# Four layers of linear attention and gated MLP, forward and backward: other orders at the seams of the forward pass, and the last output stored in quarters

## The chip, the core and the metric

The kernel runs on one core of a Trainium2 chip. That core has a matrix engine (TensorE, "PE" in the profile, with its weight loads as "PEld"), a vector engine (VectorE, "DVE"), a scalar engine (ScalarE, "ACT"), GpSimd ("POOL"), and SyncE ("SP"), which issues the DMA transfers. The engines run side by side, each through its own list of instructions in order, and wait for one another on semaphores. Results of matrix products land in PSUM, a small memory that other engines must read before a tile of it can be written again.

The metric is the time of one execution on the device in microseconds (us); what is compared is the median over executions.

## The reference

A sequence of 2048 rows of width 512 in bf16 goes through four blocks, attention, MLP, attention, MLP, with the same weights in both pairs. The output is the forward result and the gradients of the input and of five weights.

```python
def attn(x, wqkv, wo):                 # 32 heads of 16
    q, k, v = split(x @ wqkv)
    phi = lambda t: where(t > 0, t + 1, exp(t)) + 1e-6
    pq, pk = phi(q), phi(k)
    kv  = einsum("bhsd,bhse->bhde", pk, v)     # one 16x16 matrix for each head
    z   = einsum("bhsd->bhd", pk)
    num = einsum("bhqd,bhde->bhqe", pq, kv)
    den = einsum("bhqd,bhd->bhq", pq, z) + 1e-6
    return (num / den) @ wo
def mlp(x, wg, wu, wd):                # inner width 1376
    return (sigmoid(x @ wg) * (x @ wu)) @ wd

x = A_x
x = x + attn(layernorm(x)); x = x + mlp(layernorm(x))
x = x + attn(layernorm(x)); x = x + mlp(layernorm(x))
# outputs: x, and vjp(grad_out) for A_x, wqkv, wo, w_gate, w_up, w_down
```

No row can begin its attention output before the sums over all 2048 rows, kv and z, are known. So each attention has a stage that makes keys and queries of all rows, and then a stage that applies them.

## The kernel before

**Tiles.** The rows are cut into 16 tiles (`st`, 0 to 15) of 128; two neighbours form a pair (`i`, 0 to 7), four a block. The residual of every tile stays in SBUF (`k.xs`, f32). A matrix product needs its left operand with the contracted dimension on partitions, so normed rows (`h`) and normed queries (`pqn`) must be turned, in one of two ways: TensorE multiplies the 128x128 blocks by an identity into PSUM and VectorE or ScalarE copies the result to SBUF, or SyncE issues a transposing DMA from SBUF to SBUF (L1020) or from DRAM.

**Who sets the order.** The forward pass is inside a `tc.manual_schedule` for TensorE, ScalarE, VectorE and GpSimd: each of these runs its instructions in the order in which the program calls them. The order of SyncE's queue, with its loads and stores, is made by a planner. PSUM tiles come from five pools: `t`, `g` and `u` with two buffers each, `y` and `ln` with one. A matmul that takes a new tile from a pool waits until the older tile in that buffer has been read.

**Stages.** Two layer pairs follow one another, each made of `kq_fwd` (key stage and start of the attention) and `ab_fwd` (the rest of the attention, and the MLP). Then comes the backward pass, which is not touched but for its last products.

*`kq_fwd`.* For each tile: key projection (TensorE, `t_mm`), `exp_to` (ScalarE), `clamp` and `phi_out` (VectorE, the latter reads the PSUM tile and writes `pk_all`), the same for the query, then partial sums of kv. It needs the turned normed rows. In the first layer pair they are turned as it goes (`stage_hT`). In the second (l = 2) tiles 0 and 1 were turned at the end of the MLP before (`early_T`, L611), tiles 2 and 3 are turned by `stage_hT([2, 3], "vector")` in the middle of tile 0's keys, tiles 4 and 5 by `put_hT([4, 5], "vector")` in the middle of tile 2's (both with VectorE's copy from PSUM, L379), and the later ones by DMA from DRAM (`load_hT`). The turned rows are also stored for the backward pass (`store_hT`).

After the last tile the stage makes kv (`kvbdT`), folds it with wo to M (`M_sb`, four products, each copied from PSUM by ScalarE or VectorE in turn), and begins the attention of the first tiles.

*The fronts of the attention* (`attn_fronts`, L960 on). For a tile: `prod` (query times z), `front1` (VectorE's reduction to `den`), `front2` (reciprocal and `pqn`, in the buffer `pqnstage`), `front3` (four blocks turned by TensorE into the one `ln` PSUM buffer, copied by ScalarE to `pqnT`), then `attn_mm` (four products of `pqnT` with `M_sb` into `y_ps`) and `attn_add` (VectorE adds it to the residual and takes statistics for the next norm). Tiles 0 to 3 go one by one. From pair 2 on the fronts work on pairs: `pair_prod` (GpSimd), `pair_front1`, `pair_front2`. For pairs 3 to 7 `pair_front2` has `pqn` turned by two DMAs (L1020). For pair 2 (tiles 4 and 5) it is called with `turned=False`, and `pair_front3(2)` (L1033) has TensorE turn eight blocks, copied by ScalarE in one piece.

*`ab_fwd`.* The prologue takes the MLP of tiles 0 and 1 one tile at a time, with the attention of tiles 2 and 3 in between. `gu(st, nt, c0, nch)` is one unit: gate and up products (L1133, into `g_ps` and `u_ps`), two sigmoids by ScalarE, `hhT` by VectorE (which reads `u_ps`), one product by GpSimd (`ssd_t`, L1152) and its store (L1155). `stage_T` turns normed rows of coming tiles. `fill` and `fills` turn parts of the weights for the backward pass, as work for TensorE with a copy behind it. Then a loop over pairs 1 to 7 has six units per pair (`CUNITS`), with the attention of the next pair, `pair_front1` and `pair_front2` of pairs further on, and `down_mm` (the down product of a tile, L1168, followed by the residual's add and the statistics) between the units. So the turned queries of pair 2 are first used in the loop's first round (i = 1), by the attention of tiles 4 and 5 behind its first unit.

At the end, with a next layer pair to come (`nxt`): turned rows of tiles 0 and 1 (`early_T`), norm of tile 13, down product of tile 14, a block transpose by VectorE (`trans`, STREAM_TRANSPOSE in the trace), down product of tile 15, another block transpose.

*The end of the kernel.* `p2_gen` makes the weight gradients as jobs; each job is four units (`ic`, 0 to 3) of 16 matmuls into a `p_ps` tile (L1778); VectorE adds to it a part that was stored earlier, into `dw_stg`, and after the fourth unit the whole 128x4x256 result goes out in one DMA (L1732, in the helper `io`). Between the last units the main program takes steps of `a_small_grads`, which makes the small gradients of the attention weights (`sg_ps`, copied by ScalarE to `fin_o` at L2157 and stored at L2158). Its last step comes after the last unit.

## Time and profile before

| | |
|---|---|
| three executions | 1104.79, 1104.92, 1106.0 us |
| median | 1104.92 us |
| the profiled execution's own time | 1104.22 us |
| span of its profile | 1102.5 us |
| granted TensorE clock in it | 1.00 |
| busy: TensorE / VectorE / ScalarE / GpSimd | 1076.6 / 719.1 / 484.9 / 463.1 us |
| second key stage begins | 202.0 us |
| last unit of the weight gradients released to VectorE | 1097.84 us |

The span runs from the first to the last instruction of the profile; the execution's time also has what lies around it, here 1.7 us. Positions below are microseconds from the span's start. A line of a timeline gives the start, the duration, the engine, the program's line, the operation, output and inputs by their names, the shapes, a count where several equal instructions follow one another, and in square brackets the time for which the engine stood idle just before, with the instruction that released it. "SPq" is an instruction in SyncE's queue, so a DMA's line there is its issue, not its landing.

### The profile page before, as it was taken

How to read it: one execution, taken by the hardware profiler on the slowest of the kernel's cores; microseconds unless marked ns; L12 is line 12 of the kernel's file. 1: busy time of each engine (PE TensorE's matmuls, PEld its weight loads, DVE VectorE, ACT ScalarE, POOL GpSimd, SP SyncE). 2: the span in 40 equal slices, each digit the busy share in tenths (PEclk: the TensorE clock that was granted, in tenths of full speed). 3: DMA queues.
4: the chain of work that ended last, by engine and by line, in shares of the span. 5: the costliest groups of instructions: out<-in, count | busy, mean ns of one | idle time of the engine just before them, and what ended most of it. 6: DMA issues, size and time to landing. Idle time of an engine off the chain costs nothing. (4 is left out here: it accounts for less than half of the span.)

```text
span 1102.5 us, 19826 instructions
## 1 busy us (share of the span) xinstructions
PE 1076.6 (98%) x7255; PEld 660.9 (60%) x7356; DVE 719.1 (65%) x1257; ACT 484.9 (44%) x907; POOL 463.1 (42%) x631
## 2 busy tenths in 40 slices
PE   8999999999999999999999999999999999999998
PEld 4477777447777744445756556544447755555587
DVE  7798997878888667777965620067778946632221
ACT  6676555547555524444633441234346513420001
POOL 5637776435765447773101420048881102420000
PEclk9999999999999999999999999999999999999999
DMA  8948997796797688976899968898869999958997
GB/s 260 318 150 216 249 251 231 208 251 155 219 290 230 188 273 287 300 237 209 244 269 258 273 212 283 253 334 250 233 189 247 272 256 264 263 184 285 266 253 168
DMA packets 365330, 269.55 MB, mean 244 GB/s; under 512 B 132464, under 2 KB 339760, under 8 KB 365232
## 3 DMA queue, kind: packets, MB, share of 16 engines
q1 hardware_dynamic: 365232, 268.28, 85.3%
q8 instruction: 57, 0.93, 0.3%
q14 instruction: 41, 0.34, 0.1%
HBM read 122.62 MB, written 119.47 MB: 220 GB/s over the span
## 5 line engine op out<-in xcount | busy, mean ns | idle before, releaser
L1778 PE MATMUL p_ps<-p_set,p_a 128*128 128x384 bf16 (+2 forms) x1792 | 264.4, 303 | 1.5 <-DMA p_set<-sv_hdd 0.8
L1778 PEld LDWEIGHTS <-p_a 128*128 128x128 bf16 x1792 | 168.8, 96 | 85.0 <-PE p_ps L1778 1.0
L1469 POOL TENSOR_TENSOR dd<-dhb,ssd 128x512 bf16<-128x512 bf16 x84 | 97.0, 1158 | 102.9 <-ACT dhb L1467 96.3
L1468 DVE TENSOR_TENSOR dd<-dhh_ps,ssd 128x512 bf16<-128x512 f32 x85 | 57.2, 679 | 119.9 <-ACT dhb L1467 117.1
L1493 PE MATMUL dh_ps<-wuT,dd 128*128 128x512 bf16 (+1 forms) x339 | 128.5, 379 | 0.5
L1493 PE MATMUL dh_ps<-wgT,dd 128*128 128x512 bf16 (+1 forms) x329 | 124.7, 379 | 0.1
L1493 PEld LDWEIGHTS <-dd 128*128 128x128 bf16 x680 | 66.4, 98 | 79.6
L1152 POOL TENSOR_TENSOR ssd_t<-hhT,oms 128x512 bf16<-128x512 bf16 (+2 forms) x76 | 82.8, 1098 | 49.1 <-DVE hhT L1151 22.4
L1793 DVE TENSOR_TENSOR dw_stg<-p_ps,dw_stg 128x384 bf16<-128x384 f32 (+2 forms) x76 | 32.2, 438 | 105.6 <-PE p_ps L1778 96.7
L1467 ACT CAST dhb<-dhh_ps 128x512 bf16<-128x512 f32 x84 | 48.7, 589 | 115.4 <-PE dhh_ps L1461 108.1
L1133 PE MATMUL u_ps<-hT,wu 128*128 128x256 bf16 (+1 forms) x792 | 92.7, 261 | 1.2 <-DVE hhT L1151 1.0
L1133 PE MATMUL g_ps<-hT,wg 128*128 128x256 bf16 (+1 forms) x792 | 92.8, 261 | 0.7 <-DVE den L972 0.4
L1090 DVE STREAM_TRANSPOSE tr_stg<-dd 128x768 f32<-128x768 f32 (+1 forms) x62 | 86.8, 1435 | 1.5 <-DMA sv_hdd<-tr_stg 0.4
L1133 PEld LDWEIGHTS <-wg 128*128 128x128 bf16 x792 | 70.1, 98 | 17.0 <-issue 0.5
L1461 PE MATMUL dhh_ps<-gT,wdT 128*128 128x512 bf16 x299 | 76.9, 379 | 2.2 <-DVE dd L1468 1.5
L1168 PE MATMUL y_ps<-wd,hhT 128*128 128x512 bf16 (+1 forms) x337 | 77.7, 379 | 0.8
L1133 PEld LDWEIGHTS <-wu 128*128 128x128 bf16 x792 | 70.6, 98 | 9.0 <-issue 2.1
L1149 ACT ACTIVATE ssd_t<-g_ps 128x512 bf16<-128x512 f32 (+2 forms) x76 | 42.5, 559 | 63.2 <-PE g_ps L1133 60.6
L1795 ACT CAST dw_stg<-p_ps 128x384 bf16<-128x384 f32 (+2 forms) x76 | 28.1, 386 | 84.1 <-PE p_ps L1778 80.9
L1461 PEld LDWEIGHTS <-wdT 128*128 128x128 bf16 x352 | 34.2, 98 | 43.3 <-issue 3.5
L1151 DVE TENSOR_TENSOR hhT<-u_ps,ssd_t 128x512 bf16<-128x512 f32 (+2 forms) x76 | 47.2, 629 | 17.8 <-PE u_ps L1133 11.0
L1150 ACT ACTIVATE oms<-g_ps 128x512 bf16<-128x512 f32 (+2 forms) x96 | 53.7, 559 | 10.0 <-POOL ssd_t L1152 9.3
(256 smaller groups left out, 1879.8 us busy)
## 6 DMA issues: line engine op xcount, KB each, us to landing
sv_hdd<-tr_stg SPq DMA_DIRECT2D x72, 384.0 KB, 4.8
p_set<-sv_hdd SPq DMA_DIRECT2D x18, 1536.0 KB, 7.3
ssd<-sv_ssd SPq DMA_DIRECT2D x23, 768.0 KB, 5.2
sv_ssd<-ssd_t SPq DMA_DIRECT2D x61, 256.0 KB, 3.4
h_ld<-sv_h SPq DMA_DIRECT2D x30, 256.0 KB, 4.0
sv_hdl<-tr_stg SPq DMA_DIRECT2D x24, 256.0 KB, 5.1
p_a<-sv_h SPq DMA_DIRECT2D x12, 512.0 KB, 6.7
p_set<-sv_hdl SPq DMA_DIRECT2D x24, 256.0 KB, 5.0
```

The lines of the kernel that those rows point to most:

```text
L1090: nc.vector.transpose(t[:, :, 0:n * P].bitcast(F32).rearrange("p q (a j) -> p q a j", a=2 * n), src.rearrange("p c x -> p (c x)").bitcast( ...
L1133: nc.tensor.matmul(ps[:, ci * n:(ci + 1) * n], lhsT=w_sb[:, kc, (c0 + ci) * P:(c0 + ci + 1) * P], rhs=hT[:, kc, (st % 2) * P:(st % 2) * P ...
L1150: nc.scalar.activation(oms, gv, ACT.Sigmoid, scale=-1.0)
L1151: nc.vector.tensor_tensor(hh, uv, ssd[:, :, 0, :], ALU.mult)
L1152: nc.gpsimd.tensor_tensor(ssd[:, :, 1, :], hh, oms, ALU.mult)
L1168: nc.tensor.matmul(y_ps[:], lhsT=h[0:r, fc, off:off + P], rhs=k.wd[0:r, fc, :], start=(fc == 0), stop=(fc == NFC - 1))
L1461: nc.tensor.matmul(ps[:], lhsT=k.wdT[:, jc, u * P:(u + 1) * P], rhs=self.gT[B][:, jc, :], start=(jc == 0), stop=(jc == NDC - 1))
L1467: nc.scalar.copy(dhb[:], ps[:])
L1468: nc.vector.tensor_tensor(self.dd[ng][:, 0, c, :], ps[:], self.ssd[ng][:, c, 0, :], ALU.mult)
L1469: nc.gpsimd.tensor_tensor(self.dd[ng][:, 1, c, :], dhb[:], self.ssd[ng][:, c, 1, :], ALU.mult)
L1493: nc.tensor.matmul(self.acc[j][:], lhsT=dd[0:r, a, c, j * P:(j + 1) * P], rhs=w[0:r, u, :], start=(u == 0 and a == 0), stop=(u == NFC - 1 ...
L1778: nc.tensor.matmul(ps[:, 0:w], lhsT=lhs[:, s, ic * P:(ic + 1) * P], rhs=rhs, start=(s == 0), stop=(s == NST - 1))
```

## The change

It is made of these parts.

1. **Tiles 2 and 3 of the second key stage** are turned at the end of the MLP before, between the down products of tiles 14 and 15 (`early_T(1, "scalar")`), with the copy on ScalarE; the turn in the key stage is gone. `down_mm` is split so that the residual's add can be called by itself, and the end of `ab_fwd` is reordered: block transpose, down product of tile 14, turn, add, block transpose, down product of tile 15.
2. **Tiles 4 and 5 of the second key stage** are turned where they were, but copied by ScalarE.
3. **Attention tile 1** is turned after the four products for M, not before them, and copied by VectorE.
4. **In the prologue of `ab_fwd`** one weight turn (`fills(1)`) goes ahead of `front3(3)`.
5. **The queries of tiles 4 and 5** are turned by two DMAs, like those of later pairs; `pair_front3` is removed. In the first round of the loop their attention stands behind the second unit, not the first. The add of tile 0's down product goes behind tile 1's last unit.
6. **The last output** of the weight gradients leaves in four stores of 64 KB, one behind each unit, and the last step of `a_small_grads` comes ahead of the last unit.

Parts 3, 4 and 5 occur twice, once in each layer pair.

```diff
@@ main, the end of the kernel
         for i in range(last):
+            if i == last - 1:
+                next(sg, None)
             next(w2)
-            if i % 2 == 1:
+            if i % 2 == 1 and i < last - 1:
                 next(sg, None)
...
-    def early_T(self):
+    def early_T(self, pair, evac):
         k = self.k
         hT = k.lnres["hT"].tile([P, NDC, 2, P], BF16, name="hT")
-        self.transposes(hT[:], (0, 1), "vector")
-        k.nc.sync.dma_start(out=k.sv[self.l]["hT"][0, :, :], in_=hT[:].rearrange("p c n t -> p (c n t)"))
-        for st in range(2):
-            self.early[st] = hT[:, :, st, :]
+        self.transposes(hT[:], (2 * pair, 2 * pair + 1), evac)
+        k.nc.sync.dma_start(out=k.sv[self.l]["hT"][pair, :, :], in_=hT[:].rearrange("p c n t -> p (c n t)"))
+        for j in range(2):
+            self.early[2 * pair + j] = hT[:, :, j, :]
...
@@ kq_fwd
             if l == 2 and st == 0:
                 load_hT(1, (1,))
-                stage_hT([2, 3], "vector")
             elif l == 2 and st == 2:
                 hTs["cur"] = hTq[1]
-                put_hT([4, 5], "vector")
+                put_hT([4, 5], "scalar")
...
         A.prod(2, nc.vector)
         A.front1(2)
-        A.front3(1)
         phis.append(late_q(NST - 1))
         for c in range(NDC):
             m_ps = ps_tile(k, "gu"[c % 2], [P, D], F32, "M_ps")
             nc.tensor.matmul(m_ps[:], lhsT=kvbdT[:, c, :], rhs=k.wo[:, c, :], start=True, stop=True)
             evac_copy(k, A.M_sb[:, c, :], m_ps[:], "vector" if c % 2 else "scalar")
         nc.scalar.activation(k.tab[:], k.neg[:], ACT.Sigmoid)
+        A.front3(1, "vector")
         A.attn_y(0)
...
@@ pair_front2 (pair_front3 is removed)
-        if turned:
-            pqnT = pool.tile([P, 2, NDC, P], BF16, name="pqnT2", bufs=2)
-            for j in range(2):
-                nc.sync.dma_start_transpose(out=pqnT[:, j, :, :], in_=pqn[:, j, :])
-                F_[2 * i + j] = dict(T=pqnT[:, j, :, :])
+        pqnT = pool.tile([P, 2, NDC, P], BF16, name="pqnT2", bufs=2)
+        for j in range(2):
+            nc.sync.dma_start_transpose(out=pqnT[:, j, :, :], in_=pqn[:, j, :])
+            F_[2 * i + j] = dict(T=pqnT[:, j, :, :])
         nc.sync.dma_start(out=dram_batch(sva["pqn"], i, 2), in_=pqn[:])
...
@@ ab_fwd, prologue
         gu(0, 1, *CQUADS[2])
+        fills(1)
         A.front3(3)
-        fills(1)
         gu(1, 1, *CQUADS[0], between=lambda: A.attn_y(3, "t"))
         ln.apply(2)
         A.pair_front1(2)
         gu(1, 1, *CQUADS[1])
         ln.apply(3)
-        A.pair_front2(2, False)
+        A.pair_front2(2)
         A.pair_prod(3)
-        down_mm(0)
+        add = down_mm(0)
         gu(1, 1, *CQUADS[2])
+        add()
         turn_weights()
         ln.stage_T([2, 3], bank="t")
         fill("gu", "scalar")
-        A.pair_front3(2)
...
@@ ab_fwd, loop
             gu(st, 2, *CUNITS[0])
             if l == 3 and i > 1:
                 turn_weights()
-            A.attn_y(st + 2, "t")
-            A.attn_y(st + 3, "t")
+            if i > 1:
+                A.attn_y(st + 2, "t")
+                A.attn_y(st + 3, "t")
             A.pair_front1(i + 2)
             after(st - 3)
             gu(st, 2, *CUNITS[1])
+            if i == 1:
+                A.attn_y(st + 2, "t")
+                A.attn_y(st + 3, "t")
             A.pair_front2(i + 2)
...
@@ ab_fwd, end
         if nxt is not None:
-            nxt.early_T()
-        after(NST - 3)
-        down_mm(NST - 2)
-        trans(NBLK - 1, 2)
-        down_mm(NST - 1, "t")
-        trans(NBLK - 1, 3)
+            nxt.early_T(0, "vector")
+            after(NST - 3)
+            trans(NBLK - 1, 2)
+            add = down_mm(NST - 2)
+            nxt.early_T(1, "scalar")
+            add()
+            trans(NBLK - 1, 3)
+            down(NST - 1, "t")
+        else:
+            ...
...
@@ p2_gen, after the copy of each unit
+            if final and i == len(jobs) - 1:
+                nc.sync.dma_start(out=k.outs[nm][ic * P:(ic + 1) * P, c0:c0 + w], in_=ov[:, lo:lo + w])
             if post:
                 post.pop(0)()
             if ic == NDC - 1:
                 prefetch(i + 2)
             yield
+        if final and i == len(jobs) - 1:
+            continue
```

More of the change, by code (lines that the diff above doesn't have):

```diff
@@ L670, in stage_hT @@
                 return
-            if st0 % NB == 0 or (st0 == 2 and ln.early):
+            if st0 % NB == 0:
                 hTs["cur"] = stg.tile([P, 2, NDC, 2, P], BF16, name="hTst", bufs=2 if l == 0 else 3)
@@ L682, in put_hT, with store_hT @@
             if sts[-1] % NB == NB - 1:
-                store_hT(sts[-1] // NB, 1 if l == 2 else 0)
+                store_hT(sts[-1] // NB)
         hTq = {}
-        def store_hT(b, a=0):
+        def store_hT(b):
             hTs["cur"] = hTq.get(b, hTs["cur"])
-            nc.sync.dma_start(out=sv["hT"][2 * b + a:2 * b + 2, :, :].rearrange("n p x -> p n x"),
-                              in_=hTs["cur"][:, a:2, :, :, :].rearrange("p n c j t -> p n (c j t)"))
+            nc.sync.dma_start(out=sv["hT"][2 * b:2 * b + 2, :, :].rearrange("n p x -> p n x"),
+                              in_=hTs["cur"][:].rearrange("p n c j t -> p n (c j t)"))
         def load_hT(b, half=(0, 1)):
@@ L978, in front2, with front3 @@
             nc.sync.dma_start(out=dram_batch(sva["pqn"], st // 2, 2), in_=cur["pqn"][:])
-    def front3(st):
+    def front3(st, evac="scalar"):
         if st >= NST:
@@ L987, in front3 @@
         transpose_blocks(k, k.ps["ln"], pqnT, [f["pqn"][:, c * P:(c + 1) * P] for c in range(NDC)],
-                         "scalar", tag="ln_tp")
+                         evac, tag="ln_tp")
         f["T"] = pqnT
@@ L1003, in pair_front1, with pair_front2 @@
         nc.vector.tensor_reduce(f["den"][:], f["prod"][:].rearrange("p n (h e) -> p (n h) e", h=H), AX.X, ALU.add)
-    def pair_front2(i, turned=True):
+    def pair_front2(i):
         if i >= NST // 2:
@@ L1016, in pair_front2 @@
                                 rden.unsqueeze(2).to_broadcast([P, 2 * H, DH]), ALU.mult)
-        if turned:
-            pqnT = pool.tile([P, 2, NDC, P], BF16, name="pqnT2", bufs=2)
-            for j in range(2):
-                nc.sync.dma_start_transpose(out=pqnT[:, j, :, :], in_=pqn[:, j, :])
-                F_[2 * i + j] = dict(T=pqnT[:, j, :, :])
-        nc.sync.dma_start(out=dram_batch(sva["pqn"], i, 2), in_=pqn[:])
-        f["pqn"] = pqn
-    def pair_front3(i):
-        if i >= NST // 2:
-            return
-        pqn = F_[2 * i]["pqn"]
-        pqnT = pool.tile([P, 2, NDC, P], BF16, name="pqnT2", bufs=2)
-        ps = ps_tile(k, "ln", [P, 2, NDC, P], BF16, "ln_tp")
-        for j in range(2):
-            for c in range(NDC):
-                nc.tensor.transpose(ps[:, j, c, :], pqn[:, j, c * P:(c + 1) * P], k.ident[:])
-        nc.scalar.copy(pqnT[:], ps[:])
-        for j in range(2):
-            F_[2 * i + j] = dict(T=pqnT[:, j, :, :])
-    A.pair_prod, A.pair_front1, A.pair_front2, A.pair_front3 = pair_prod, pair_front1, pair_front2, pair_front3
+        pqnT = pool.tile([P, 2, NDC, P], BF16, name="pqnT2", bufs=2)
+        for j in range(2):
+            nc.sync.dma_start_transpose(out=pqnT[:, j, :, :], in_=pqn[:, j, :])
+            F_[2 * i + j] = dict(T=pqnT[:, j, :, :])
+        nc.sync.dma_start(out=dram_batch(sva["pqn"], i, 2), in_=pqn[:])
+    A.pair_prod, A.pair_front1, A.pair_front2 = pair_prod, pair_front1, pair_front2
     def attn_mm(st, bank="y"):
@@ L1169, in down_mm, with add, down @@
                                  start=(fc == 0), stop=(fc == NFC - 1))
-            nc.vector.tensor_tensor(k.xs[st][:], y_ps[:], k.xs[st][:], ALU.add)
-            if nxt is not None:
-                nxt.stats(st)
+            def add():
+                nc.vector.tensor_tensor(k.xs[st][:], y_ps[:], k.xs[st][:], ALU.add)
+                if nxt is not None:
+                    nxt.stats(st)
+            return add
+        def down(st, bank="y"):
+            down_mm(st, bank)()
         def after(st):
@@ L1242, in ab_fwd @@
             if i > 1:
-                down_mm(st - 2)
+                down(st - 2)
             ln.apply(st + 2)
@@ L1249, in ab_fwd @@
                 turn_weights()
-            down_mm(st - 1, "t")
+            down(st - 1, "t")
             ln.apply(st + 3)
@@ L1275, in ab_fwd @@
         if nxt is not None:
-            nxt.early_T()
-        after(NST - 3)
-        down_mm(NST - 2)
-        trans(NBLK - 1, 2)
-        down_mm(NST - 1, "t")
-        trans(NBLK - 1, 3)
+            nxt.early_T(0, "vector")
[7 more added lines that the diff above has]
+        else:
+            after(NST - 3)
+            down(NST - 2)
+            trans(NBLK - 1, 2)
+            down(NST - 1, "t")
+            trans(NBLK - 1, 3)
         if out_cb is not None:
```

## The prediction

> **What bounds the kernel now.** I read the page, then who TensorE waited for, then the timelines of the seams that the diff touches, then SyncE's queue with the landings of its transfers. The page first:

> ```profile
> span 1102.5 us, 19826 instructions
> PE 1076.6 (98%) x7255; PEld 660.9 (60%) x7356; DVE 719.1 (65%) x1257; ACT 484.9 (44%) x907; POOL 463.1 (42%) x631
> ```

> TensorE is busy for all but 26 us, so a change can only remove matrix work or close one of a few holes. TensorE's waits (line waited for: us in total, times, longest) name those in reach:

> ```profile
> PE t_mm L704 <- DVE pk_all L738: 2.5, 4, 1.2
> PE u_ps L1133 <- DVE hhT L1151: 1.0, 2, 0.6
> PE ln_tp L372 <- DVE pqnstage L974: 0.7, 2, 0.3
> PE y_ps L1046 <- ACT M_sb L381: 0.6, 2, 0.3
> PE t_mm L704 <- DVE hTst L379: 0.4, 1, 0.4
> ```

> First and last are the second key stage, the others the two attention-to-MLP seams. The span was 1102.5 us and that execution's own time 1104.22 us, 1.7 us around it; the median shown is 1104.92 us, 0.7 us more. My sum is a difference in the profiled span, applied to the median. A measurement of this kernel tells about 0.2% (2.2 us) from no change.

> **Second key stage.** Its timeline, two stretches:

> ```profile
> 206.50 1.04 PE L704 MATMUL t_mm<-wqkv,hTst 128*128 128x512 bf16 x4 [0.42 <-DVE hTst L379]
> ...
> 210.06 0.68 DVE L379 COPY hTst<-hT_tp 128x1024 bf16<-128x1024 bf16 x1
> ...
> 210.97 0.69 DVE L738 SCALAR_TENSOR_TENSOR pk_all<-t_mm,ak_t 128x512 bf16<-128x512 f32 x1
> ...
> 211.72 1.02 PE L704 MATMUL t_mm<-wqkv,hTst 128*128 128x512 bf16 x4 [1.21 <-DVE pk_all L738]
> ```

> VectorE enters the stage late: two residual adds, two STREAM_TRANSPOSEs (1.52 and 1.08), then the copy of tiles 2 and 3 (0.68 at 205.75) and of tiles 4 and 5 (0.68 at 210.06). TensorE stands still for the first copy, then at 211.72 for a PSUM tile that pk_all of tile 2 must release. The change gives both copies to ScalarE, which takes 1.01 for such a copy (hT, 82.53), and puts tiles 2 and 3 between the last two down projections. I replay it with these rows. The eight transposes (0.45) move from 202.9 to 199.64, so TensorE loses nothing; their copy lies on ScalarE at about 200.3, which then waits for its next matmul until 203.08. VectorE: STREAM_TRANSPOSE 199.1 to 200.6, add and statistics of tile 14 to 202.2, STREAM_TRANSPOSE to 203.35, tile 15 to 205.0, first key clamp at 205.0 instead of 206.36. Each tile then takes 0.28+0.69+0.28+0.69 and gaps, which puts pk_all of tile 2 at 210.0 instead of 211.66. TensorE reaches that wait at 209.6, stands to 210.06, and begins tile 4's keys at 211.57 (it also needs the query tile that VectorE releases at 211.0); before, it began them at 213.22. Gain 1.65. Bounds: 0.7 if only one copy's 0.68 comes back, 1.9 if the rest of the wait closes too. I take the replay. From tile 4 on a tile costs TensorE 2.38 (eleven matmuls of 0.216) and VectorE 1.9 to 2.2, so it is kept. What is late next is ScalarE: its second copy stands ahead of the exponential of tile 2's queries, ending at 209.7, 0.1 ahead of VectorE's turn.

> [...]

> **The end.** SyncE's queue there:

> ```profile
> 1098.30 0.38 SPq L1732 DMA_DIRECT2D out_dram<-dw_stg  x1
> 1098.33 0.59 ACT L2157 CAST fin_o<-sg_ps 128x512 bf16<-128x512 f32 x1 [3.35 <-PE sg_ps L2154]
> 1098.94 0.33 SPq L2158 DMA_DIRECT2D out_dram<-fin_o  x1
> ```

> The two stores land at 1100.63 and 1101.41, and 1.1 us of closing follow. After the change the small product goes ahead of the last unit, whose last matmul then ends at 1098.09 (same work); VectorE starts 0.2 later, takes 0.42, and a 64 KB quarter is issued at 1098.75. The nearest row is a lone 128 KB store of fin_o, 1.7 from issue to landing at 1095.0: landing at 1100.45, gain 0.95. Bounds: 1.4 faster if 64 KB lands in 1.25, nothing if it takes the 2.5 of the old last store. Three further stores queue in the 4 us units before it.

> [...]

> **Attention seams (layer pairs 0/1 and 2/3).** *M_sb.* Turning tile 1 after the four M products removes the 0.31 wait at 58.46, but the next reader, y_ps of tile 0, waits for M_sb, and VectorE's half of those copies starts only at 60.19, after a reduction that ends at 60.10. So only 0.1 in the first pair, nothing in the second; VectorE's new copy of 0.42 fills its idle 0.52 and 0.47 before the residual add. Bounds: 0.3 either way.

> *Fill before front3(3).* TensorE turns a weight (0.22, or 0.16 for three blocks) while VectorE ends pqnstage: gain 0.2 each, up to the next step.

> *Tiles 4 and 5.* What this hangs on:

> ```profile
> 82.53 1.01 ACT L381 COPY hT<-ln_tp 128x1024 bf16<-128x1024 bf16 x1
> 83.01 0.62 PE L1033 MATMUL ln_tp<-ident,pqnstage 128*128 128x128 bf16 x8
> 83.60 1.03 PE L1133 MATMUL g_ps<-hT,wg 128*128 128x256 bf16 x8
> 85.00 1.03 PE L1133 MATMUL u_ps<-hT,wu 128*128 128x256 bf16 x8 [0.37 <-DVE hhT L1151]
> ```

> Sixteen transposes in all vanish, 0.45 per pair, but they save nothing: the matmuls behind them need hT, copied until 83.54, and start at 83.60. The add moved behind hhT does free u_ps, 0.54 in the first pair; in the second u_ps did not wait, and what goes is a wait of about 0.3 for the ScalarE copy of pqnT at 275.2. So TensorE would reach tile 4's attention at 86.87 (before the 0.2 it would be 87.09), or 276.64. Now the new wait. SyncE's queue:

> ```profile
> 82.08 2.70 SPq L1155 DMA_DIRECT2D sv_ssd<-ssd_t  x2
> 84.87 0.81 SPq L1022 DMA_DIRECT2D sv_pqn<-pqnstage  x1
> ```

> The two turns take the place at 84.87, behind two ssd stores. The second of these waits for a GpSimd product that takes 2.1 instead of 1.16 while VectorE writes pqnstage, so I put the first turn at 84.65, and 274.05 in the second pair. One turn occupies the queue for 1.25 and lands 2.5 after its issue:

> ```profile
> L1020 SPq DMA_TRANSPOSE pqnT<-pqnstage x20: 1189/1254/2275, 94.3 to 348.6; - x20
> ...
> DMA to landing us min/median/max: 2.4/2.5/4.5
> ```

> Tile 5 lands 3.75 after the first issue, at 88.4 and 277.8. With 0.1 to wake and 0.86 of products the next unit starts at 89.4 and 278.8, against 89.35 and 278.68 before. Moving the attention behind the second unit thus just covers the DMA: with busy queues ahead in the first pair (that pqn store took 0.81 to issue) I take 0.2 lost there and 0.1 in the second. Queued behind the waiting matmuls is all of TensorE; behind the turns on SyncE, the pqn store and one ssd store, which nobody reads soon. Bounds per pair: 0.75 gained if the turns are in time, 2.2 lost at the slowest pair of rows (158.86 issued, 2.28 in the queue, the second landing 3.6 after its own issue: 5.9).

> Sum: -1.65 -0.95 -0.1 +0.2 +0.1 = **-2.4 us**, so 1102.5 by the median. The backward pass follows TensorE and its loads wait for buffers that TensorE frees, so it shifts as a whole.

> **Rivals.**
> *The turn comes late.* Of ten pairs of turns six land within 3.8 us of the first issue; one took 5.4 and one 5.9. The loss is that time less 3.7 in each layer pair, and it decides against the whole change from 5.05 in both, where two losses of 1.35 eat the other 2.7. At 5.9 in both: 2.2+2.25-2.7 = +1.75, 1106.7; in one, 1104.5. For it: loaded queues near 84; against: the short rows are the common ones. [...]

> *ScalarE takes VectorE's place in the key stage.* If its two copies delay the exponentials, only 0.7 comes back there: sum -1.45, 1103.5. For it: the margin of 0.1 above; against: ScalarE idles 3.26 before the first exponential.

> *The turn comes early.* Were GpSimd's product not held up, the store ahead would go about 1 us sooner, and each pair gains up to 0.75: sum -4.2, 1100.7. For it: both engines' order shifts here; against: VectorE's pqnstage still precedes the product's end in both layer pairs.

> **How the numbers follow.** Forecast 0.50, its own range 1101.6 to 1103.3, two thirds of it beyond 0.2%; early turn 0.17; ScalarE 0.15, most of it within 0.2%; late turn 0.18, 0.07 of it slower by over 0.2%, where a slow turn meets small gains elsewhere. Faster: 0.33+0.17+0.03 = 0.53; slower 0.07; same 0.40. Range from all edits at their good ends, 1100.4, to one slow turn with a small key gain, 1105.6.

> **What would show it.** Right: no DVE copy of hTst in the key stage, the 1.21 wait down to about 0.5, tile 4's keys 1.65 earlier; y_ps of tile 4 and 5 waiting for DMA pqnT, 0.3 to 0.4 each; the last store a quarter, landing 1.7 after issue. Wrong: no DMA wait at y_ps (then it is faster), one over 1.5 (then not), ScalarE named as releaser of t_mm, or a last store that lands after 2.5.

## The result: slower by 0.2%, and the profile after

The changed kernel's median is 1107.03 us over 16 executions (1105.52 to 1109.51), the kernel before's 1104.88 (1104.25 to 1106.0). The ratio is 1.0021, 95% interval 1.0013 to 1.0029: 2.15 us slower, where 2.4 faster was forecast. Two later comparisons of the same pair gave 1.0012 (1.0003 to 1.0021) and 1.0025 (1.0014 to 1.0035).

The page of after. Its execution took 1109.24 us, one of the slowest of the 16, so its span says more than the median does:

```profile
span 1107.5 us, 19807 instructions
PE 1078.0 (97%) x7241; PEld 661.1 (60%) x7340; DVE 717.5 (65%) x1257; ACT 483.3 (44%) x905; POOL 464.0 (42%) x631
```

TensorE is busy 1.4 us longer and the span is 5.0 longer: most of the time is in waits. Those of TensorE (us in total, times, longest):

```profile
PE y_ps L1032 <- DMA pqnT<-pqnstage: 2.7, 3, 1.5
PE dhh_ps L1465 <- DVE dd L1472: 2.4, 6, 0.5
PE p_ps L1782 <- DMA p_set<-sv_dq: 2.2, 1, 2.2
PE t_mm L706 <- DVE pk_all L740: 1.8, 4, 0.8
PE ln_tp L374 <- DVE pqnstage L975: 0.4, 1, 0.4
```

The first line is the new wait for the turned queries. The next two lie in the backward pass, whose code is unchanged but for its last products. The last two are what was left of the waits that the change aimed at. The second key stage's timeline:

```profile
207.64 1.01 ACT L383 COPY hTst<-hT_tp 128x1024 bf16<-128x1024 bf16 x1
...
210.15 1.02 PE L706 MATMUL t_mm<-wqkv,hT 128*128 128x512 bf16 x4 [0.54 <-DVE pk_all L740]
...
211.66 1.03 PE L706 MATMUL t_mm<-wqkv,hTst 128*128 128x512 bf16 x4
```

The wait of 1.21 is 0.54, and tile 4's keys start at 211.66 instead of 213.22. At the end, the last quarter is one DMA:

```profile
1104.46 0.42 DVE L1797 TENSOR_TENSOR dw_stg<-p_ps,dw_stg 128x256 bf16<-128x256 f32 x1 [1.77 <-PE p_ps L1782]
1104.91 0.33 SPq L1801 DMA_DIRECT2D out_dram<-dw_stg  x1
```

It landed at 1106.44, 1.53 after its issue. And the two places where the queries of tiles 4 and 5 are used, with the turn's issue ahead of the first:

```profile
84.00 3.19 SPq L1020 DMA_TRANSPOSE pqnT<-pqnstage  x2
...
88.06 1.67 PE L1032 MATMUL y_ps<-M_sb,pqnT 128*128 128x512 bf16 x7 [1.47 <-DMA pqnT<-pqnstage]
...
276.47 0.81 PE L1032 MATMUL y_ps<-M_sb,pqnT 128*128 128x512 bf16 x3 [0.97 <-DMA pqnT<-pqnstage]
...
277.53 1.04 PE L1032 MATMUL y_ps<-M_sb,pqnT 128*128 128x512 bf16 x4 [0.25 <-DMA pqnT<-pqnstage]
```

The pair of turns took 3.19 us in SyncE's queue, where the working had 2.5.

Where the 5.0 us arise is seen by matching TensorE's instructions one by one between two profiles. The table gives by how much the same instruction starts later (+) than in before's profile; the last column is an experiment told below.

| instruction (its start before) | after | after, list 32 longer |
|---|---|---|
| kv of the first layer pair (57.26) | -0.20 | -0.07 |
| behind the products for M (61.80) | -0.44 | -0.31 |
| gate product of tile 1 (74.40) | -0.66 | -0.54 |
| up product of tiles 2, 3 (85.44) | -1.20 | -1.07 |
| unit behind tiles 4 and 5 (89.78) | +0.22 | -0.41 |
| last turn ahead of the key stage (196.81) | -0.16 | -0.81 |
| end of the key stage (240.04) | -1.59 | -1.66 |
| second pair, up product (274.18) | -1.46 | -1.81 |
| unit behind tiles 4 and 5 (279.55) | -0.27 | -1.34 |
| first product of the backward pass (384.67) | -0.27 | -1.34 |
| first weight-gradient unit (506.28) | +0.96 | -1.34 |

So in this profile the forward pass loses at the two places of tiles 4 and 5 most of what it had gained, and the backward pass adds more, although, up to its last products, it runs the same instructions in the same order on every engine.

### The profile page after: what moved, and what is told of

It reads as the page before. It is cut to its first block, busy times and chain, and to the rows that moved or that the text cites. A ratio compares the mean times of both kernels' runs of the same rounds, so it can differ in the third digit from the quotient of the medians.

```text
span 1107.5 us, 19807 instructions
## 1 busy us (share of the span) xinstructions
PE 1078.0 (97%) x7241; PEld 661.1 (60%) x7340; DVE 717.5 (65%) x1257; ACT 483.3 (44%) x905; POOL 464.0 (42%) x631
```

## The experiments

All ratios are to the kernel before, run in turn on the same chip, with 95% intervals.

**One: which part.** The first kernel undoes part 5's turns and order (the moved add stays), the next three make one part alone.

```diff
 # e1_no_turn: after.py, with
+        A.pair_front2(2, False)      # no DMA turn
+        A.pair_front3(2)             # eight blocks by TensorE, copy by ScalarE
+            A.attn_y(st + 2, "t"); A.attn_y(st + 3, "t")   # behind the first unit, all i
 # e2_turn_only: before.py, with part 5's turns, order and moved add
+        A.pair_front2(2)
+        add = down_mm(0)
         ...
+        add()
 # e3_key_only: before.py, with the two copies of the key stage
+            trans(NBLK - 1, 2)
+            add = down_mm(NST - 2)
+            nxt.early_T(1, "scalar")
+            add()
         ...
+                put_hT([4, 5], "scalar")
 # e4_end_only: before.py, with the small product ahead of the last unit, and the quarters
+            if i == last - 1:
+                next(sg, None)
         ...
+            if final and i == len(jobs) - 1:
+                nc.sync.dma_start(out=k.outs[nm][ic * P:(ic + 1) * P, c0:c0 + w], in_=ov[:, lo:lo + w])
```

> The changed kernel with tiles 4 and 5 of both layer pairs turned by TensorE again and their attention back behind the loop's first unit; all else of the change stays. Theory 'turn' (the wait of TensorE for the two DMA turns costs 0.9 us in the first layer pair and 1.2 in the second by the profile after, and the rest of the change gains): 1104.9 -1.4 key stage -0.66 fronts -0.5 freed u_ps -0.95 end = about 1101.4. Rival 'given back' (what the forward pass gains is lost at the backward pass's first loads, which came 1.2 us late in the profile after): 1104 to 1105. Rival 'end' (quarter stores and the earlier small product cost 2 us at the end): about 1104.4.

> The kernel before with only part 5: tiles 4 and 5 turned by DMA, their attention behind the second unit, the add of tile 0 behind tile 1's last unit. Theory 'turn': waits of 1 to 1.5 us for pqnT in each layer pair, +0.9 and +1.2, so about 1107.0. Rivals 'given back' and 'end': the turn is a small part, 1105.0 to 1105.5.

> The kernel before with only parts 1 and 2: tiles 2 and 3 turned at the end of the MLP before, both copies of the second key stage by ScalarE. Theory 'turn': the key stage gains 1.4, about 1103.5, and the shift carries through the backward pass. Rival 'given back': 1104.5 to 1105.2, with the key stage 1.4 earlier and the backward pass as late as before.

> The kernel before with only part 6: last output in quarter stores and the last step of the small gradients ahead of the last unit. Theory 'turn': 0.95 gained at the end, about 1103.9. Rival 'end': 1 to 2 us lost, 1106 to 1107. Rival 'given back' says nothing of it: there is nothing behind the end, so 1103.9 too.

Measured: without the turns 0.9955 (0.9942 to 0.9967), that is 5.0 us faster than before; part 5 alone 1.0040 (1.0026 to 1.0054), 4.4 slower; the key stage alone 0.9984 (0.9975 to 0.9993), 1.8 faster; the end alone 0.9987 (0.9978 to 0.9996), 1.4 faster. Part 5 is the loss, and the other parts gain what the sum gave them or more. The rivals 'given back' and 'end' fall. But the profiles give part 5 only some 2 us in the forward pass: the backward pass's first product starts at 384.40 in after and at 382.66 without the turns (the later profiles have 384.14 and 386.08 for after and 382.20 without them, so the difference is 1.5 to 3.9, where the ratios are 7 us apart).

**Two: is it the wait?** After and before again, the version without turns again, and one in which 2.5 us of work that has to be done anyway stands ahead of the attention of tiles 4 and 5.

```diff
 # f3_cover: after.py, with
             if i == 1:
+                down(st - 1, "t")
                 A.attn_y(st + 2, "t")
 ...
-            down(st - 1, "t")
+            if i > 1:
+                down(st - 1, "t")
```

> The changed kernel once more, unaltered, for a second profile and for a comparison on one chip with the three others. Theory 'turn' (TensorE's wait for the two turns is the loss): the forward pass again about 2.2 us behind the version without the turns, with waits for pqnT of 1 us or more in both layer pairs; time 1.002 of before. Theory 'load' (beside the wait, the turns disturb what follows, since the version without them was 7 us faster and the waits explain only 2.2): the forward pass 2.2 behind, the time 5 to 7 behind.

> The kernel before once more, for a second profile: how far the waits of the backward pass for its loads differ between two executions of one kernel. Theory 'turn': by 1 to 3 us in the sum of TensorE's waits for p_set and dd, as between the other profiles. Theory 'load': by less than 1 us, all of it within 0.1% of the first.

> The changed kernel with tile 1's down product (2.5 us of TensorE work) put ahead of the attention of tiles 4 and 5 in the loop's first round, so that the DMA turns land behind work that has to be done anyway. Theory 'turn': no wait for pqnT is left, the forward pass is 2.2 us faster than the changed kernel's and the time within 1 us of the version without DMA turns. Theory 'load': the wait goes, 2.2 us come back, and 3 us or more are still missing to the version without DMA turns.

> The version without the DMA turns of tiles 4 and 5 once more, on the same chip as the changed kernel. Theory 'turn': faster than the changed kernel by 2 to 3.5 us. Theory 'load': by 5 to 7 us, with a backward pass that is shorter by 3 us or more in its profile.

Measured: after 1.0012, before against itself 1.0001 (0.9992 to 1.0009), without turns 0.9964 (0.9952 to 0.9976), covered 1.0019 (1.0009 to 1.0030). The covered version came out where neither theory had put it. Of the waits at tiles 4 and 5 one of 0.8 was left, but another took their place; in TensorE's waits, and in the first pair:

```profile
PE u_ps L1119 <- DVE hhT L1137: 3.1, 3, 1.6
```

```profile
96.50 0.60 PE L1119 MATMUL u_ps<-hT,wu 128*128 128x256 bf16 x4 [1.56 <-DVE hhT L1137]
```

Three residual adds with their statistics, and a pqnstage behind them, now stood together on VectorE ahead of hhT, which TensorE needs to get u_ps back. As a test of 'wait' this run is inconclusive.

**Three: the transfers, and an earlier turn.** In one kernel TensorE turns the queries and the DMA turns are issued all the same; in the next the turns go ahead of the store that waits for GpSimd. The third splits the end part.

```diff
 # g1_spare_turns: e1_no_turn, in pair_front2
+        else:
+            spare = pool.tile([P, 2, NDC, P], BF16, name="pqnT2", bufs=2)
+            for j in range(2):
+                nc.sync.dma_start_transpose(out=spare[:, j, :, :], in_=pqn[:, j, :])
 # g2_early_turns: after.py, the ssd store of gu(1, 1, *CQUADS[1]) held back
+        held = gu(1, 1, *CQUADS[1], hold=True)
         ...
         A.pair_front2(2)
+        with tc.issue_after(A.turn):
+            held()
 # g3_quarters_only: before.py, with the last output in quarters and nothing else
+            if final and i == len(jobs) - 1:
+                nc.sync.dma_start(out=k.outs[nm][ic * P:(ic + 1) * P, c0:c0 + w], in_=ov[:, lo:lo + w])
```

> The version without the DMA turns (tiles 4 and 5 turned and used by TensorE's way), but the two DMA turns of each layer pair are issued all the same, at the changed kernel's place in SyncE's queue, into a buffer that nobody reads. No engine waits for them. Theory 'wait' (the loss is TensorE's waiting and what it shifts): as fast as the version without them, 0.996 of before, within 1 us. Theory 'load' (the transfers themselves disturb what follows): 2.5 to 5 us slower than that version, 0.998 to 1.001 of before, with a forward pass as early as that version's.

> The changed kernel, with the two turns and the store of pqn put ahead of the one ssd store that waits for GpSimd. The turns are issued when VectorE ends pqnstage, 1.0 to 1.5 us sooner. Theory 'wait': the waits for pqnT shrink from 1.2 to 0.3 or less in each layer pair, the forward pass is 1.8 us ahead of the changed kernel's, and the time falls by 2 to 4 us, to 0.998 of before. Theory 'load': the forward pass gains the 1.8 and the time no more than that, about 0.9995.

> The kernel before with the quarter stores alone; the last step of the small gradients stays behind the last unit, so its fin_o store is the last transfer. If the last store's landing sets the end: that 128 KB store landed 0.78 after the big one, so nothing is gained, 1.0000 within 0.0005. If the big store's 512 KB held up the one behind it: up to 0.7 us gained.

Measured: spare turns 0.9964 (0.9951 to 0.9976), so with TensorE's turns in place the transfers cost nothing, and 'load' falls. Early turns 1.0005 (0.9996 to 1.0013), and of TensorE's waits for the turned queries only this was left:

```profile
PE y_ps L1032 <- DMA pqnT<-pqnstage: 0.6, 1, 0.6
```

Its forward pass ended at 383.53, 0.4 us behind that of the spare turns (383.12), yet its time was 3.9 us longer (medians 1106.3 and 1102.43). So 'wait' falls too, as the whole of the loss. Quarters alone: 1.0003 (0.9994 to 1.0012), nothing, because the fin_o store was still behind them; part 6 needs both its halves.

**Four: TensorE's list.** No version so far without the sixteen transposes (32 instructions of TensorE, with their weight loads; after's page has 16 weight loads fewer than before's, 7340 for 7356) was faster than before; of the changed versions with as long a list all were, but for the quarters alone. One kernel puts the transposes back without using their result; one moves the attention without a DMA; one makes part 5 in the first layer pair alone.

```diff
 # h1_spare_transposes: after.py, with
         fill("gu", "scalar")
+        A.spare_front3(2)    # eight transposes of pqn into an ln_tp tile that nobody reads
 # h2_order_only: e1_no_turn, with the later attention
+            if i > 1:
                 A.attn_y(st + 2, "t"); A.attn_y(st + 3, "t")
         ...
+            if i == 1:
+                A.attn_y(st + 2, "t"); A.attn_y(st + 3, "t")
 # h3_first_pair: after.py in layers 0/1, e1_no_turn in layers 2/3
+        A.pair_front2(2, la == 0)
         ...
+        if la == 2:
+            A.pair_front3(2)
```

> The changed kernel, in which TensorE also turns the eight blocks of tiles 4 and 5 as before, into a PSUM tile that nobody reads, at the place where it stands waiting for hT (0.65 us). The attention still waits for the DMA turns. TensorE's list is then as long as that of the version without DMA turns. Theory 'wait': nothing changes, 1.001 of before, 4 to 5 us behind the version without DMA turns. Rival 'list' (the backward pass is slower because 32 fewer instructions stand ahead of it on TensorE): the forward pass stays, the time falls by 2 to 3 us, 0.999.

> The version without DMA turns, but with the attention of tiles 4 and 5 behind the second unit as in the changed kernel. Theory 'wait': 0.996 to 0.997 of before, as without this move, since no engine waits for a DMA. Rival 'order' (the later attention, not the DMA, costs the time in and behind the forward pass): 0.999 to 1.001.

> The changed kernel with the DMA turns and the later attention in layer pair 0/1 only; pair 2/3 turns by TensorE. Theory 'wait': each pair costs by its own wait; 0.7 of the 2.2 us of the forward pass lie in the first pair, 1.4 in the second, so a third of the loss remains, 0.9975 to 0.9985. Rival 'list': half of it, as half of the 32 instructions are missing.

> The changed kernel a third time, beside the three others on one chip. All theories: 1.001 to 1.002 of before; waits for pqnT of 2.3 to 2.7 us in sum, with the second turn landing 4.0 to 4.6 us after the first one's issue.

Measured: spare transposes 0.9984 (0.9975 to 0.9992), order only 0.9963 (0.9950 to 0.9977), first pair only 0.9985 (0.9975 to 0.9994), after 1.0025. Sixteen unused transposes made the changed kernel 4.3 us faster (1108.29 to 1103.95). The later attention costs nothing. With TensorE's list shorter by 16 only, the time lies between.

**Five: the list, far from the seam.** The spare transposes could have helped by keeping TensorE from standing still. So the list is lengthened where nothing else changes, in the warm-up before the first real product, and shortened there in a version that gained. The last 24 of the longer warm-up are 32 columns wide instead of 128, so that it ends no later.

```diff
 # j1_after_plus32: after.py; j3_no_turn_plus32: e1_no_turn; both with
-            for i in range(WARM):
-                nc.tensor.matmul(warm_ps[:], lhsT=k.ident[:], rhs=k.ident[:], start=True, stop=True)
+            for i in range(WARM + 16):
+                n = P if i < 30 else 32
+                nc.tensor.matmul(warm_ps[:, 0:n], lhsT=k.ident[:], rhs=k.ident[:, 0:n], start=True, stop=True)
 # j2_no_turn_minus32: e1_no_turn, with
-WARM = 38
+WARM = 22
```

> The changed kernel, its seams untouched; only the warm-up at the very start, before TensorE's first real matmul, has 54 small matmuls for 38 (30 of 128 columns and 24 of 32), about as long as before. TensorE's list is 32 instructions longer, so from the first seam to the end every instruction has the place in the list that it has in the version without DMA turns (off by 16 between the two seams). Theory 'list' (where TensorE's instruction fetches of 256 instructions fall decides how late loads land): 0.9980 to 0.9995 of before, 3 to 4 us faster than the changed kernel, as with the spare transposes. Rival 'idle' (the spare transposes helped because TensorE did not stand still at hT): 1.001 to 1.0025, as the changed kernel.

> The version without DMA turns, but with 22 warm-up matmuls for 38 at the very start, so that TensorE's list is 32 instructions shorter, as the changed kernel's is behind the second seam. Theory 'list': 2 to 4 us slower than with 38, 0.998 to 1.000 of before. Rival 'idle': 0.996 as with 38, or up to 0.5 us off by the first microseconds.

> The version without DMA turns with 54 warm-up matmuls as in the first of these three: a third place for the fetches. Theory 'list': another time than 0.996, by up to 3 us to either side. Rival 'idle': 0.996, within 0.5 us.

Measured: the changed kernel with a list 32 longer 0.9966 (0.9953 to 0.9979), 1101.78 us; the version without turns with a list 32 shorter 1.0012 (1.0004 to 1.0021); with one 32 longer 0.9975 (0.9966 to 0.9983), a third place with a third time, though not clear of the noise. The changed kernel needed only 16 more warm-up matmuls to go from 1.0012, 1.0021 or 1.0025 (its three comparisons) to 0.9966, and the version that gained lost it all when 16 were taken away. About 1.7 us of the latter are its own: with the short warm-up TensorE stood still for 1.40 us and its first products ran at half speed, 1.89 us for four instead of 1.03 (below); that leaves about 4 us by the ratios. A single profile says less: its backward pass, from the first product to the end, took 721.0 us, against 716.2 to 719.8 in the four profiles with 38 and the queries turned by TensorE (e1, f4, g1, h2). The place in the list is the cause of 4 to 6 us; 'idle' falls. TensorE's waits and both places of tiles 4 and 5 in the changed kernel with the longer list, where the lines' numbers are one higher:

```profile
PE y_ps L1033 <- DMA pqnT<-pqnstage: 0.8, 2, 0.4
...
PE dhh_ps L1466 <- DVE dd L1473: 0.7, 2, 0.5
```

```profile
87.10 2.01 PE L1033 MATMUL y_ps<-M_sb,pqnT 128*128 128x512 bf16 x8 [0.38 <-DMA pqnT<-pqnstage]
...
275.60 1.90 PE L1033 MATMUL y_ps<-M_sb,pqnT 128*128 128x512 bf16 x8 [0.45 <-DMA pqnT<-pqnstage]
```

The two waits are near the 0.3 to 0.4 that the working had, and the waits for dd in the backward pass are a third of what they were in after (0.7 for 2.4; before has 1.5).

**What lies between the list and the loads.** The profile counts the transfers that fetch instructions apart. After's line of that queue (packets, MB, share of the time of 16 DMA engines):

```profile
q8 instruction: 57, 0.93, 0.4%
```

That is 57 packets of 16 KB, one for about every 256 of TensorE's instructions (14581 with the weight loads): in the profiles of before and after a packet begins each time 254 more of the recorded ones have begun, on average. In the trace's record of packets each takes 0.88 to 2.11 us in after and 0.88 to 1.56 in before; the page counts them on the same 16 DMA engines as the data. Their times show what a shift of 32 instructions does:

| | profiles | fetch begins | measured |
|---|---|---|---|
| second pair's turns, first issue to second landing | after (three profiles), part 5 alone, covered | within 0.2 us of the first issue | 4.00 to 5.12 |
| the same | early turns | 1.9 us after it, during the turns | 4.36 |
| the same | spare turns, spare transposes, after with the list 32 longer | 0.9 to 2.5 us before it | 3.75 to 3.78 |
| ssd load issued 7.4 us behind the backward pass's first product | seven with a list 32 short (after three times, e2, f3, g2, j2) | 9.6 to 10.1 us behind that product, inside the load | landed 5.98 to 6.57 after issue |
| the same | all thirteen others | 2.5 to 5.4 us behind it, ahead of the load | 5.45 to 5.86 |

The groups do not overlap. In the first layer pair it is less clear: the fetch had ended by the first turn's issue in nine of ten profiles (in one of them 0.03 us after it), and the pair took 3.86 to 4.41; in the tenth, with the early turns, it ran over the issue (82.8 to 84.5, issue 83.14), and the pair took 5.13.

The packets' record allows the same comparison for the whole backward pass. All 20 profiles have 419 of its transfers (the outputs left out). For each, the question is whether a fetch overlaps the shortest time that the transfer took in any profile, counted from its issue. For 120 of them that is so in at least four profiles and not so in at least four others: 100 of the 120 landed later, by the median, with the fetch than without, and the median of all 120 differences is 0.80 us. In 23 the two groups do not overlap, and in each of these the transfers with a fetch are the later ones.

That the place of the instructions decides is shown by the fourth and fifth steps above. That transfers land later beside a fetch is shown by these comparisons. How it comes about was not shown: which engine a packet used is not recorded, and no run moved a fetch without moving the list. Nor is the sum of 4 to 6 us traced wait by wait: the later waits for p_set differ between executions of one kernel by 1 to 2 us. Open too is why the unused transposes (0.9984) did less than the longer warm-up (0.9966); their waits for pqnT were 0.81 and 0.78 us.

By the measurements, the place of TensorE's instructions among these 57 packets was worth 4 to 6 us of 1105.

## Why the prediction was wrong, by its own steps

- **Second key stage, -1.65.** Right in kind. No VectorE copy of hTst is left, the wait at tile 2 is 0.54 (0.5 was worked out), and tile 4's keys start 1.40 sooner once the 0.16 already gained is taken off. VectorE reached the stage's first clamp at 204.46, ahead of the 205.0 that was worked out, but its first pk_all then stood 0.66 us for a store of tr_stg to land, which is more than the missing 0.25. To the stage's end -1.43 remains. Alone it measured 1.8, of 0.8 to 2.8.
- **The end, -0.95.** Right. The last quarter landed 1.53 after issue, not 1.7. From the start of VectorE's last copy to the span's end it is 3.07 us instead of 4.67; the small product that now stands ahead takes 0.45 of these 1.60, so 1.15 is gained. Alone it measured 1.4, of 0.4 to 2.4.
- **M_sb, -0.1, and the fill, 0.2.** -0.24 and -0.22 in the first pair. In the second pair M_sb gave nothing that lasted, as said, and the fill's 0.2 did not come either. The 0.54 at u_ps came back to the hundredth (1.20 less 0.66).
- **Tiles 4 and 5, +0.2 and +0.1.** This term was mis-sized. The time of two turns was taken as 3.75; it was 4.41 and 4.59 in after. By the table of starts, the first pair lost 0.88 from the gate product of tile 1 to the unit behind tiles 4 and 5, and the second 1.19 from its up product to that unit. With 32 instructions added to the list the same two turns took 3.90 and 3.78, near the row, and TensorE waited 0.38 and 0.45.
- **"Sixteen transposes in all vanish ... but they save nothing."** The failing step. They were priced by the work that hides them, at nothing. Their absence makes TensorE's list 32 instructions shorter and so moves the later instruction fetches (the one behind the backward pass's first product began 10.1 us after that product in after, 3.9 in before), and that place in the list costs 4 to 6 us, more than all the rest gains.
- **"The backward pass follows TensorE ... so it shifts as a whole."** It did not. With the median 2.15 above before, the forward pass 0.27 ahead in this profile, and 1.15 gained at the end, some 3.6 us were lost in between, an estimate that joins a median to one profile.
- **The rivals.** The late turn was the nearest: the lag came out between its short and its long rows, but its point of decision, 5.05 in both pairs, was not reached, and by itself it would have left the kernel faster. ScalarE as the bound did not occur: neither copy of it released TensorE in the second key stage. The early turn was no rival of its own: issued a microsecond sooner (g2), it gave 1.0005 and no gain over before. Once the list was as long, turning by DMA and turning by TensorE were worth the same within their intervals, 0.9966 and 0.9963.

The whole change, with the list kept at its length, gives 0.9966: 3.8 us less, of 2.3 to 5.2, where the sum said 2.4. The versions that leave the queries with TensorE have 0.9955, 0.9964 and, with the later attention, 0.9963, medians of 1101.04 to 1101.48 us. These, and the changed kernel with the longer list, beat both kernels, and their intervals do not tell them apart.

## What to carry to other kernels

Here 32 instructions fewer on TensorE moved its later instruction fetches, and loads far from the edit landed later with them (the ssd load 5.98 to 6.57 us after its issue, instead of 5.45 to 5.86). Where a kernel is tuned to a few microseconds in a thousand, compare two versions at equal list lengths (some spare matmuls where the engine has nothing to do are enough) before the difference is credited to the edit. And a wait that is covered by moving work in front of it should be looked up on the other engines too: here the cover's own residual add stood in VectorE's way and gave the time back, with a wait of 1.56 us for hhT.

## What the runs showed of the hardware that was not expected

```profile
1070.61 5.27 PE L1782 MATMUL p_ps<-p_set,t_a 128*128 128x256 bf16 x32 [2.19 <-DMA p_set<-sv_dq]
```

```profile
1066.63 3.65 PE L1778 MATMUL p_ps<-p_set,t_a 128*128 128x256 bf16 x32 [0.40 <-DMA p_set<-sv_dq]
```

  Stretches of 1 us (busy time of each engine, then granted clock, DMA share, GB/s):

```profile
1069.00:1070.00 1.00, 0.00 (x0) 0.00 (x0) 0.00 (x0) 0.00 (x0) 0.00 (x0) 1.00 0.29 78
...
1072.00:1073.00 1.00, 1.00 (x7) 0.67 (x5) 0.00 (x0) 0.00 (x0) 0.00 (x0) 0.50 1.04 297
...
1074.00:1075.00 1.00, 1.00 (x11) 0.90 (x10) 0.42 (x1) 0.00 (x0) 0.00 (x0) 1.00 1.19 292
```

  These 32 matmuls took 5.27 us, where before's took 3.65: the stall cost 1.6 us on top of itself. It is one reason why this profile is among the slowest. The profile of the version without turns with 54 warm-up matmuls (j3) has the same: a stand of 2.59 us, and the clock at half for 3.41. The waits of up to 1.5 us at tiles 4 and 5 left the clock at 1.00, and so did a stand of 1.69 in g2. In after the record of the granted clock has it at half for 3.41 us, from 1070.53.
- **With a shorter warm-up full speed came later.** With 22 matmuls TensorE stood for 1.40 us behind them and then ran at half speed to about 11 us. The record of the granted clock begins only at 10.68 us there, with 1.00 (at 5.58 in after's profile and 4.24 in before's, both with 38 matmuls); the views show 1.00 ahead of that too, where there is no record:

```profile
6.76 1.89 PE L706 MATMUL g_mm<-wqkv,hTst 128*128 128x512 bf16 x4
```

  The next groups of four took 1.91 us from 8.44, 1.29 from 10.15 and 1.03 from 11.28; in after's profile four took 1.03 from 7.52 on.
